# Sliding-window attention with a GELU feed-forward on one core: all output stores issued from ScalarE's queue

## The chip, the core and the metric

The kernel runs on one core of a Trainium2 chip. The metric is the device time of one execution in microseconds (us), the median of the runs. The profile is one execution on the same core, read by engine: TensorE (PE, with its weight loads PEld), VectorE (DVE), ScalarE (ACT), GpSimd (POOL) and the sync engine (SP), which computes nothing and only issues transfers. A `q` after an engine's name (SPq, ACTq) marks its instruction queue: issuing a transfer or waiting for one.

## What is computed

Attention over a causal window of 64 positions, for 8 batches of 8 heads, 576 positions and 64 elements per head; its output, taken as 4608 tokens of 512 elements, goes through a feed-forward layer with a quick GELU.

```python
scores = scale * np.matmul(q, k.transpose(0, 1, 3, 2))
mask = (rel >= 0) & (rel < window)                # rel = i - j, window = 64
attn = softmax(np.where(mask, scores, -1e9))
x = np.matmul(attn, v)  -> 4608 x 512
h = x @ w_in                                      # 512 x 2048
out = (h / (1.0 + np.exp(-1.702 * h))) @ w_out    # 2048 x 512, float32
```

## The kernel before, in words

The 4608 tokens are nine chunks of 512. A chunk's way is: q and k are loaded as bf16 (`load_bf16`, step `l`, on GpSimd's queue) and turned by a DMA transpose on the sync queue (`turn_dma`, step `y`, L240, two transfers `qt` and `kt` for each row block). TensorE makes scores (`c`, L319) into PSUM, ScalarE the exp (`x`, L333 or L335), VectorE the mask (`m`, L339), TensorE the product with v (`v`, L347), VectorE the normalised rows `xs` (`n`, L392). These are turned into `xT`, from chunk 4 on by a DMA transpose on the sync queue (`x_dma`, step `t`, L437).

The feed-forward layer then works in units `u` (L453): eight matmuls into one of two PSUM buffers `hps`, each emptied by ScalarE with a gelu (`.g`, L484) or, with a tanh first (`.t`, L464), by VectorE (`g`, L479). Since the same two buffers serve all units, TensorE is never more than two units ahead of ScalarE. The gelu and the exp need different tables on ScalarE; `soften` (L1089) and the first gelu after an exp bring a table load each.

The second matrix product is done for pairs of 128-token blocks with seven products instead of eight (`p`, L568): "chain" and "part" are its two PSUM banks, `k` copies a partial chain into SBUF (`keep_chain`, L113), `o` adds a half of an output row block into `o_sb` (`add_out`, L593, VectorE) and `z` copies the last half (`last_of_chain`, L113). `o_sb` has five buffers. When both halves are there, step `s` stores 128 rows of 512 float32 (256 KB, `store`, L584). In step names such as `s3.1` the first number is the pair (two to a chunk), the second the block in it; the last chunk has some stores in halves.

Chunks 0 and 1 are written out step by step; from chunk 2 on the order is the string `plan`, a list of such steps that the last lines of the kernel run one after the other. Each engine gets its own instructions in this order and works through them in order. Across engines only semaphores hold: one for each computing engine, and eight (DMAHW0 to DMAHW7) that the transfers of the sync queue and of ScalarE's queue use in turn. A transfer adds to its semaphore when it has landed. Before a transfer is issued, its queue waits for its data and for the landing of the transfer that had the same semaphore before, eight places earlier in the turn.

The plan around two of the stores, cut at the points:

```python
    u60.g p4.3 o4.3 a5.3 h4.1 a5.1 s3.1 l5.0 y4.2 h4.2 p4.4 z4.V x18 p5.1 ... k5.1.A u61.t ... p5.2 c19
    u93.g s6.0 p8.7 k8.7.V l6.4 p8.5 a8.4 c26 x26 c27.h x27 p8.4 ... y6.2 l7.1 z8.V p9.1 a9.1 s8.1 m26 y6.4 u94.t c28
```

The choice of queue is the first line of `store`: chunks below 6 and the second halves of the last chunk go to the sync queue, the others to ScalarE's. The stores of chunk 0 (`down_out`, L507) have a line of their own.

Of the kernel before, what the change touches and what calls it, by code (L numbers as in the profile page):

```python
# [29 lines left out]
def kernel(  # L30
# [9 lines left out]
    nc = tc.nc  # L40
# [538 lines left out]
        return o_of[c, pr, t][:, 256 * n : 256 * n + 256]  # L579

    def store(c, pr, t, half=None):
        eng = nc.sync if c < 6 or half == 1 else nc.scalar
        cols = slice(0, DM) if half is None else slice(256 * half, 256 * half + 256)
        eng.dma_start(  # L584
            out=out_tiled[:, 4 * c + 2 * pr + t, cols], in_=o_of[c, pr, t][:, cols]
        )
# [523 lines left out]
    def turn(m):  # L1110
# [15 lines left out]
        "o": lambda q, n: add_out(*pair(q), n),  # L1126
        "z": lambda q, e: last_of_chain(*pair(q), engines[e]),
        "s": lambda q, *t: store(*pair(q), *t),
        "a": lambda q, *n: add_g(*pair(q), *n),
        "w": add_w,  # L1130
# [48 lines left out]
```

The softmax here doesn't subtract the row's maximum and nothing guards it: scores larger than these inputs give would overflow.

## Time and profile before

| what | before |
|---|---|
| time, median of 3 runs (lowest, highest) | 295.31 us (294.74, 299.89) |
| span of the profiled execution | 293.0 us |
| ScalarE, gelu L484: 82 of them, mean | 597 ns |
| ScalarE, exp of 128x1024, L335: 28, mean | 1017 ns |
| ScalarE, table loads: 22, mean | 1283 ns |
| stores L584 on the sync queue: 22, median issue | 530 ns |
| stores L584 on ScalarE's queue: 12, median issue | 338 ns |
| DMA transposes on the sync queue: 80 | 60 at L240, 20 at L437 |

The page gives for each engine its busy time and share of the span. A list of waits says which instruction stood idle and what ended that, with total, times and longest in us. The timeline is a list of instructions with start and duration in us, and in brackets the idle time before one and what ended it. A line of the view by stages gives, after the length, the busy time of PE, PEld, DVE, ACT and POOL with the number of instructions, then the granted TensorE clock, the mean load of the 16 DMA engines (over 1 where packets of several queues are open on one engine at a time) and GB/s. Issuing a transfer is not counted as busy.

The 14 stores L584 issued before 205 us took 3.1 to 8.5 us from issue to landing; the 12 of ScalarE's queue, all after 246 us, 1.7 to 2.8 us.

### The profile page before, as it was taken

The page shows a single profiled execution, that of the slowest core. Times are in us where ns is not written, and L with a number is a line of the kernel's source. Part 1 is how long each engine was busy: PE and PEld are TensorE (multiplying, and loading weights), DVE is VectorE, ACT ScalarE, POOL GpSimd, SP SyncE. Part 2 cuts the span into 40 slices and gives each one's busy share as a digit, 9 for nine tenths or more (in the row PEclk, how much of TensorE's full clock was granted, in tenths as well). Part 3 has the DMA queues.
Part 4 walks back from the last instruction along what each step waited for, and adds up shares of the span by engine and source line. Part 5 has one row for each costly group of instructions (what it writes and reads, how often), then busy time and mean ns, then how long its engine had stood idle before and what let it go on. Part 6 is the DMA issues. An engine that isn't in the chain of part 4 may idle for free.

```text
span 293.0 us, 8976 instructions
## 1 busy us (share of the span) xinstructions
PE 283.5 (97%) x3783; PEld 249.6 (85%) x3783; DVE 195.5 (67%) x377; ACT 181.1 (62%) x289; POOL 141.3 (48%) x191
## 2 busy tenths in 40 slices
PE   7899999999999999999999999999999999999995
PEld 6578555999898898889898999998899899989984
DVE  5667715898898685375636573756787864768771
ACT  3676534877775389776758746776657653556411
POOL 1570446744999999709569985078510000000000
PEclk9999999999999999999999999999999999999999
DMA  7999999996999999999999999999955171001233
GB/s 237 236 206 219 240 243 225 239 159 128 84 142 119 166 130 134 185 164 146 140 186 154 139 151 198 183 160 143 142 70 117 36 182 39 0 2 72 74 125 126
DMA packets 149768, 42.79 MB, mean 146 GB/s; under 512 B 135136, under 2 KB 144864, under 8 KB 149728
## 3 DMA queue, kind: packets, MB, share of 16 engines
q0 software_dynamic: 77712, 13.64, 70.7%
q1 hardware_dynamic: 68208, 25.18, 49.4%
q10 hardware_dynamic: 3808, 3.41, 3.7%
q8 instruction: 29, 0.48, 0.7%
q14 instruction: 11, 0.09, 0.1%
HBM read 36.70 MB, written 9.44 MB: 157 GB/s over the span
## 4 chain that ended last, share of the span: by engine, by line
PE 78%; DMA 10%; DVE 4%; ACT 2%; SPq 2%; issue 2%; POOL 1%; ACTq 0%; DVEq 0%; POOLq 0%
PE hps L453 32%; PE chain L568 17%; PE part L568 13%; PE ops L491 5%; PE up L668 4%; DMA out_dram<-o_sb 3%; PE Tacc L347 3%; PE S L319 3%; DMA kt<-rows_k 3%; DMA stage_v<-in_v_dram 2%; DMA stage_qk<-in_k_dram 2%; SPq L240 1%; DVE stage_qk L528 1%; ACT PT L335 1%; PE turn L196 1%
## 5 line engine op out<-in xcount | busy, mean ns | idle before, releaser
L453 PEld LDWEIGHTS <-w_in_sb 128*128 128x128 bf16 x1312 | 109.6, 113 | 4.9 <-issue 0.7
L484 ACT ACTIVATE gT<-hps 128x512 bf16<-128x512 f32 x82 | 48.6, 597 | 34.5 <-PE hps L453 34.2
L453 PE MATMUL hps<-xT_pe,w_in_sb 128*128 128x128 bf16 (+2 forms) x800 | 61.0, 234 | 0.1
L453 PE MATMUL hps<-xT_dma,w_in_sb 128*128 128x256 bf16 x512 | 60.6, 273 | 0.3 <-ACT gT L694 0.3
L568 PEld LDWEIGHTS <-gT 128*128 128x128 bf16 x512 | 49.0, 98 | 5.9
L479 DVE SCALAR_TENSOR_TENSOR gT<-th,hps 128x512 bf16<-128x512 bf16 x46 | 30.8, 684 | 11.2 <-ACT th L464 11.0
L233 POOL COPY v_off<-v_nat 64x528 bf16<-64x528 bf16 x27 | 20.2, 752 | 33.9 <-DMA v_nat<-in_v_dram 33.1
L464 ACT ACTIVATE th<-hps 128x512 bf16<-128x512 f32 x46 | 27.0, 600 | 13.0 <-PE hps L453 12.6
L593 DVE TENSOR_TENSOR o_sb<-part,stage_v 128x256 f32<-128x256 f32 x48 | 20.2, 421 | 21.9 <-PE part L568 13.3
L335 ACT ACTIVATE PT<-S 128x1024 bf16<-128x1024 f32 x28 | 28.5, 1017 | 8.0 <-PE S L319 7.6
L339 DVE TENSOR_TENSOR PT<-PT,band_all 128x1024 bf16<-128x1024 bf16 x32 | 23.6, 748 | 5.6 <-ACT PT L335 5.4
L229 POOL DMA_DIRECT2D v_nat<-in_v_dram x27 | 23.5, 871 | 0.8 <-DMA rows_q<-in_q_dram 0.5
L228 POOL DMA_DIRECT2D rows_k<-in_k_dram x27 | 23.3, 865 | 0.3 <-DMA v_nat<-in_v_dram 0.3
L228 POOL DMA_DIRECT2D rows_q<-in_q_dram x27 | 23.1, 856 | 0.0
L568 PEld LDWEIGHTS <-sums 128*128 128x128 bf16 x192 | 18.6, 98 | 3.2 <-issue 1.1
L568 PEld LDWEIGHTS <-stage_v 128*128 128x128 bf16 x192 | 18.5, 98 | 2.2
L113 ACT COPY stage_v<-chain 128x256 f32<-128x256 f32 x22 | 8.2, 372 | 18.3 <-PE chain L568 18.3
L392 DVE TENSOR_TENSOR xs<-Tacc,rc 128x128 bf16<-128x128 f32 (+1 forms) x26 | 18.0, 692 | 0.9
L113 DVE COPY stage_v<-chain 128x256 f32<-128x256 f32 x26 | 10.9, 420 | 11.1 <-PE chain L568 10.9
L235 POOL COPY v_off<-v_nat 64x528 bf16<-64x528 bf16 x21 | 17.2, 820 | 1.2
L568 PE MATMUL chain<-stage_qk,sums 128*128 128x256 bf16 x128 | 16.6, 273 | 0.3 <-DVE stage_v L113 0.3
L568 PE MATMUL chain<-stage_qk,gT 128*128 128x256 bf16 x128 | 16.6, 273 | 0.0
(127 smaller groups left out, 450.6 us busy)
## 6 DMA issues: line engine op xcount, KB each, us to landing
out_dram<-o_sb SPq DMA_DIRECT2D x24, 256.0 KB, 4.7
rows_q<-in_q_dram POOLq DMA_DIRECT2D x21, 128.0 KB, 6.3
rows_k<-in_k_dram POOLq DMA_DIRECT2D x21, 128.0 KB, 6.7
v_nat<-in_v_dram POOLq DMA_DIRECT2D x21, 128.0 KB, 7.4
out_dram<-o_sb ACTq DMA_DIRECT2D x10, 256.0 KB, 2.1
stage_v<-in_v_dram SPq DMA_DIRECT2D x9, 256.0 KB, 6.7
stage_qk<-in_q_dram SPq DMA_DIRECT2D x4, 512.0 KB, 6.9
stage_qk<-in_k_dram SPq DMA_DIRECT2D x4, 512.0 KB, 8.0
```

The lines of the kernel that those rows point to most:

```text
L113: (nc.scalar.copy if engine is nc.scalar else engine.tensor_copy)(**kw)
L228: nc.gpsimd.dma_start(out=heads(row_block(b, i, w)), in_=rows_of(src, b, i))
L229: nc.gpsimd.dma_start(out=v_nat[b % 2][0 : size(i), i, :, 0:D], in_=rows_of(v, b, i))
L233: nc.gpsimd.tensor_copy(out=vo[64:128, i, :, :], in_=vn[0:64, i, :, :])
L335: nc.scalar.activation(out=e[:], in_=st[:], func=AF.Exp, scale=scale)
L339: nc.vector.tensor_tensor(out=pt, in0=pt, in1=band_all[:], op=ALU.mult)
L453: nc.tensor.matmul(ps[:, g, :], lhsT=w_in[:, c, (f + g) % 4 : 512 : 4], rhs=xT[ch][:, m0 : m0 + nt // P, c, :], start=(c == 0), stop=(c == 3),
L464: nc.scalar.activation(out=th[:], in_=ps[:], func=AF.Tanh, scale=1.702)
L479: nc.vector.scalar_tensor_tensor(out=g_of(*unit), in0=th[:], scalar=1.0, in1=ps[:], op0=ALU.add, op1=ALU.mult,)
L484: nc.scalar.activation(out=g_of(*unit), in_=ps[:], func=AF.Gelu_apprx_sigmoid, scale=2.0)
L568: nc.tensor.matmul(out[:, :], lhsT=left[:, j], rhs=right[:, j], start=new and j == 0, stop=j == 7, skip_group_check=True,)
L593: nc.vector.tensor_tensor(out=out_half(c, pr, t, half), in0=C_of[c, pr][:], in1=kept(c, pr, at), op=ALU.add)
```

## The change

All stores of step `s` are issued from ScalarE's queue. The place of each store in the plan is as it was, and the stores of chunk 0 (L507) stay on the sync queue. The sync queue is then left with loads and transposes, so that no transpose stands behind a store that waits for its data, and the stores have a queue of their own on the DMA engines.

```diff
     def store(c, pr, t, half=None):
-        eng = nc.sync if c < 6 or half == 1 else nc.scalar
+        eng = nc.scalar
         cols = slice(0, DM) if half is None else slice(256 * half, 256 * half + 256)
         eng.dma_start(
             out=out_tiled[:, 4 * c + 2 * pr + t, cols], in_=o_of[c, pr, t][:, cols]
```

In the built kernels the instructions of TensorE, VectorE and GpSimd are the same and in the same order. ScalarE has 22 transfers more among its instructions, the sync engine 22 fewer. The turn of the eight semaphores changes with it; the listing of ScalarE's instructions in the changed build has, for instance, for the stores of s3.1, s6.0, s8.1 and s8.0:

```
L584 DMACopy out_dram<-o_sb 128x512 [waits DMAHW7_49,Activation_49]
L584 DMACopy out_dram<-o_sb 128x512 [waits DMAHW4_49]
L584 DMACopy out_dram<-o_sb 128x512 [waits DMAHW5_49,DVE_49]
L584 DMACopy out_dram<-o_sb 128x512 [waits DMAHW6_49,DVE_49]
```

By the values waited for, the transfers eight places before them are the first transposes of y4.2 and y6.4 for s3.1 and s6.0, the second of y6.4 for s8.1, and the first of y7.1 for s8.0.

## The prediction

> **What bounds the kernel now.** I read the page's first part for the busy shares, then busy time by stage, then the waits of TensorE, and only then the sync queue and ScalarE in time.
>
> ```profile
> PE 283.5 (97%) x3783; PEld 249.6 (85%) x3783; DVE 195.5 (67%) x377; ACT 181.1 (62%) x289; POOL 141.3 (48%) x191
> ```
>
> TensorE is busy 97% of the span, ScalarE 62%. By stage (core line: length, then busy us of each engine):
>
> ```profile
> 100.00:140.00 40.00, 39.44 (x568) 35.84 (x569) 25.16 (x49) 30.25 (x46) 29.99 (x38) 1.00 2.10 155
> 140.00:180.00 40.00, 39.88 (x493) 36.80 (x491) 23.06 (x45) 26.86 (x41) 32.72 (x41) 1.00 2.03 161
> 180.00:220.00 40.00, 39.51 (x529) 36.01 (x527) 27.57 (x55) 27.20 (x40) 17.24 (x22) 1.00 1.42 142
> ```
>
> In these 120 us, where 14 of the moved stores lie, TensorE is idle for 0.56 + 0.12 + 0.49 = 1.2 us. So nothing there can be won by more than that, and any time TensorE is made to wait is added to the end. Its waits, all of them:
>
> ```profile
> PE S L319 <- DMA kt<-rows_k: 0.5, 1, 0.5
> PE part L568 <- DVE o_sb L593: 0.5, 1, 0.5
> ...
> PE hps L453 <- ACT gT L694: 0.3, 1, 0.3
> ```
>
> So today ScalarE holds TensorE up almost never; it is ScalarE that waits (34.2 us at L484 and 12.6 us at L464 for `hps`). The question is how late ScalarE may become before that turns round.
>
> **What the skill says.** "DMA: Bandwidth & Descriptors", section "Issuing engines are not separate DMA queues": transfers from any engine run on the same 16 DMA engines, so another queue saves only the issuing time. The trace agrees as far as it goes: a store's issue took 530 ns on the sync queue and 338 ns on ScalarE's (medians of L584), the bytes are the same. "Perfetto Trace Analysis", section on the HWDGE DMA instruction: the wait for semaphores is the sequencer's, and lies before the reported start. That matters most here: a store that waits holds the whole instruction stream of its engine. The sync queue's waits show it (one L584 store sat 28.7 us behind a transfer, harmlessly).
>
> **The change, part by part.** Twenty-two stores leave the sync queue for ScalarE's; twelve were there. No work is added or removed on TensorE, VectorE, GpSimd.
>
> *Issuing.* 22 x 338 ns = 7.4 us on ScalarE. Its 181.1 us become 188.5 of some 293, and it has gaps of 0.28 us before most gelu steps. Bounds: 0 (all in gaps) to 7.4 us (all exposed). Most stores stand where ScalarE waits for TensorE afterwards anyway, so I take 1.0 us.
>
> *New waits.* In the built program each transfer of sync and ScalarE counts on one of eight landing semaphores in turn and waits for the transfer that used it before. The listing of the changed build puts the moved stores later in this turn than in step order: step s3.1 waits for the first transpose of y4.2, step s6.0 for the first of y6.4, though both follow them in the plan. Before, the store was issued first. I set each store's place on ScalarE (end of the instruction before it) against the time its data and its semaphore were ready in the trace of before. For 20 of 22 both were ready, or are ready after a wait already counted (s8.1 and s8.0 wait for the transposes just behind y6.4's first), or late by little at the tail. Two are not:
>
> ```profile
> 118.67 3.59 SPq L437 DMA_TRANSPOSE xT_dma<-xs  x2
> 122.35 0.53 SPq L584 DMA_DIRECT2D out_dram<-o_sb  x1
> 122.98 1.38 SPq L240 DMA_TRANSPOSE qt<-rows_q  x1
> ```
>
> First, s3.1 (the middle line; start, then duration). ScalarE reaches it when the gelu before ends, at 123.5:
>
> ```profile
> 122.91 0.60 ACT L484 ACTIVATE gT<-hps 128x512 bf16<-128x512 f32 x1 [0.28 <-PE hps L453]
> 123.52 1.28 ACT L1089 ACT_TABLE_LOAD   x1
> 124.81 0.20 ACT L1089 ACTIVATE gate<-gate 1x1 f32<-1x1 f32 x1
> 124.92 1.00 ACT L335 ACTIVATE PT<-S 128x1024 bf16<-128x1024 f32 x1
> ```
>
> Without the store ahead of it the y4.2 transpose starts at 122.3. The 30 qt transposes landed 2.3/5.7/8.6 us after issue (least, median, most), this one after 7.9. With 5.7 it lands at 128.0 and ScalarE stands still for 128.0 - 123.5 = 4.5 us (bounds: 1.1 with 2.3; 6.7 with 7.9). Behind it stand the table load, the exp of pair 18, the copy of chain 5.1, the tanh of unit 61. TensorE needs the exp first: scores 19 write the bank that it reads, and began at 127.81, while the exp ended at 125.92, a slack of 1.9. So TensorE loses 4.5 + 0.34 - 1.9 = 2.9 us (0 to 5.1).
>
> ```profile
> 181.27 1.29 SPq L240 DMA_TRANSPOSE kt<-rows_k  x1
> 184.71 0.33 SPq L584 DMA_DIRECT2D out_dram<-o_sb  x1
> 185.14 1.28 SPq L240 DMA_TRANSPOSE qt<-rows_q  x1
> ```
>
> Second, s6.0. It was issued at 173.7 on the sync queue; ScalarE comes to it at 181.6, after unit 93. The y6.4 transpose is the last line above. It stood behind the store of s8.1, which waited for VectorE until 184.7; now it can go at 182.6. With 5.7 us it lands at 188.3: ScalarE waits 6.7 us (2.3: 3.3; its own 7.5: 8.5). TensorE works on through the products of pairs 8 and 9 and scores 26 and 27 until unit 94, begun at 185.80, which needs the bank that the exp of pair 27 frees (first half done at 184.5): slack 1.3. Loss 6.7 + 0.34 - 1.3 = 5.7 us (2.3 to 7.5). The shift of the first loss moves ScalarE and the sync queue alike here, since that stretch of transposes starts from `xs` (L437, 176.2), which VectorE writes.
>
> *Buffers of o_sb.* s9.0 goes out at 222.7 instead of 220.7; z11 and o11.5 want its buffer at 223.8, and a store on ScalarE lands after 2.1 us (median; 1.7 to 2.8). So VectorE is late by about a microsecond and TensorE's product 11.3 (225.15) by some 0.5 us (0 to 1).
>
> *What is saved.* VectorE waited 3.9 us for s2.0's landing (issued 114.31, landed 8.4 us later behind transposes), which cost TensorE its 0.5; on ScalarE it goes at 111.5. And the kt wait of 0.5 at 204.3 falls away, as the sync queue runs ahead. Together -1.0 us (0 to -1.2, the idle time above).
>
> *Tail.* The last half stores wait in ScalarE's stream for VectorE (288.38), so the copy of z16 slips from 287.1 to 288.7 and the last copy, z17, from 289.7 to 289.8: +0.1.
>
> **Sum:** 2.9 + 5.7 + 1.0 + 0.5 - 1.0 + 0.1 = 9.2 us on 295.3: **304.5 us**, slower by 3.1%.
>
> **Rivals.**
> 1. *The transposes land in time.* Without 22 stores in the sync ring, transposes land nearer 2.3 us than 5.7. For it: the qt and kt transposes after 208.9 landed within 2.4 to 4.5 us of their issue, when GpSimd's loads were nearly done. Against: in the stages of the two waits these loads overfill the 16 DMA engines (the next to last figures above, 2.10, 2.03 and 1.42), and they stay. Losses 0 + 2.3, less 1.0: 296.6 us, no change.
> 2. *Faster.* The sync queue no longer stops behind stores that wait for VectorE, transposes come earlier, q, k and xT are never late. For it: 20.3 us of waits of L584 on VectorE. Against: TensorE waits 0.5 us for transposes in all. 295.3 - 1.0 = 294.3 us, not slower.
> 3. *ScalarE becomes the bound.* The blocks take their longest (5.1 + 7.5) and issuing half shows (3.7): 295.3 + 16.3 + 0.5 + 0.1 = 312 us. For it: 21 table loads of 1283 ns crowd just where stores stand. Against: 46.8 us of ScalarE's waiting for `hps` can take them up.
>
> **How the numbers follow.** Forecast (two blocks, each costing TensorE some us): 0.60. Rival 1: 0.25. Rival 2: 0.05. Rival 3: 0.10. Most of the forecast's own spread lies over 301.2 us (2%): 0.56; with rival 3, slower 0.66. Within 2%: rival 1, most of rival 2, the low end of the forecast, 0.32. Over 2% faster would need 5.9 us, of which TensorE has 1.2 idle in the middle: 0.02. The range, 296.5 to 311, takes in rival 1 and the forecast with its bounds, and leaves out rival 2 and the upper half of rival 3.
>
> **What would show it.** In the changed profile: a gap of ScalarE of about 4.5 us before the table load after unit 60 and of about 6.7 us after unit 93, ended by a qt transpose's landing; TensorE idle near 3 us at scores 19 and near 6 us at unit 94, and with these two its waits on ScalarE up from 0.3 to some 9 us. VectorE's 3.9 us wait on `out_dram` gone. Wrong, if ScalarE's gaps there stay under 2 us, or if they come and TensorE does not stop; if more than a third of the loss lies outside the two places, issuing or buffers were sized wrongly.

## The result, and the profile after

| | before | after |
|---|---|---|
| time, median (lowest, highest) | 295.31 us (294.74, 299.89) | 306.53 us (305.50, 307.39) |
| span of the profiled execution | 293.0 us | 303.8 us |

The ratio is 1.0371, with a 95% interval from 1.0298 to 1.0443: slower by 11.2 us. Here and below, medians and ranges are of all runs, ratios of fast runs alone, since some runs of a kernel take over 1.5% longer than its fastest. The forecast was 304.5 us. The busy shares of the page of the kernel after say where to look:

```profile
PE 284.4 (94%) x3778; PEld 250.2 (82%) x3783; DVE 196.3 (65%) x377; ACT 180.8 (60%) x289; POOL 138.4 (46%) x191
...
PEclk9999999999999999969999999999999999999999
```

TensorE's busy time is up by only 0.9 us, in a span that is 10.8 us longer: it stands idle. The second line is its granted clock in slices of 7.6 us; the lone 6 lies between 129 and 137 us. The same three stages as before (length, busy us of PE, PEld, DVE, ACT and POOL, then clock, DMA load and GB/s):

```profile
100.00:140.00 40.00, 33.48 (x457) 29.32 (x457) 20.54 (x40) 24.70 (x37) 30.25 (x40) 0.91 2.02 149
140.00:180.00 40.00, 40.00 (x519) 36.89 (x514) 23.60 (x45) 29.24 (x45) 27.80 (x37) 1.00 2.01 154
180.00:220.00 40.00, 37.72 (x511) 34.19 (x509) 23.77 (x48) 24.51 (x37) 19.88 (x25) 1.00 1.32 141
```

TensorE's idle time there is 6.5, 0.0 and 2.3 us instead of 0.6, 0.1 and 0.5, and the clock of the first stage is 0.91 instead of 1.00. The list of TensorE's waits names the cause (total, times, longest):

```profile
PE S L319 <- ACT PT L335: 5.7, 1, 5.7
PE hps L453 <- ACT PT L333: 2.5, 2, 2.3
...
PE S L319 <- DMA kt<-rows_k: 0.6, 1, 0.6
```

The first two are waits for ScalarE, at scores 19 and at unit 94. Next, ScalarE in time around the two stores (start, duration, and in brackets the idle time before):

```profile
124.37 0.60 ACT L484 ACTIVATE gT<-hps 128x512 bf16<-128x512 f32 x1 [0.28 <-PE hps L453]
131.54 0.34 ACTq L584 DMA_DIRECT2D out_dram<-o_sb  x1
131.91 1.28 ACT L1089 ACT_TABLE_LOAD   x1 [6.94 <-DMA qt<-rows_q]
...
133.31 1.00 ACT L335 ACTIVATE PT<-S 128x1024 bf16<-128x1024 f32 x1
...
188.78 0.60 ACT L484 ACTIVATE gT<-hps 128x512 bf16<-128x512 f32 x1 [0.28 <-PE hps L453]
192.77 0.34 ACTq L584 DMA_DIRECT2D out_dram<-o_sb  x1
193.14 1.28 ACT L1089 ACT_TABLE_LOAD   x1 [3.76 <-DMA qt<-rows_q]
```

The gelu of unit 60 ends at 124.97, and nothing runs on ScalarE until the store of s3.1 goes out at 131.54: 6.9 us between the gelu and the table load (the store's own issue of 0.34 included), ended by a qt transpose. The transposes behind which the two stores wait were issued here (sync queue; start, then duration of the issue), the first right behind the `xT_dma` pair:

```profile
120.14 3.59 SPq L437 DMA_TRANSPOSE xT_dma<-xs  x2
123.83 1.26 SPq L240 DMA_TRANSPOSE qt<-rows_q  x1
...
189.24 1.19 SPq L240 DMA_TRANSPOSE qt<-rows_q  x1
```

(The line of 123.83 is the first transpose of y4.2, that of 189.24 the first of y6.4.) They landed at 131.5 and 192.75 us, 7.6 and 3.5 us after their issue. And what it does to TensorE:

```profile
127.67 1.04 PE L568 MATMUL part<-w_out_sb,gT 128*128 128x256 bf16 x8
134.36 0.61 PE L319 MATMUL S<-qt,kt 64*128 64x64 bf16 x16 [5.66 <-ACT PT L335]
134.90 1.89 PE L568 MATMUL chain<-stage_qk,stage_v 128*128 128x256 bf16 x8
```

Eight matmuls of 128x256 take 1.04 us ahead of the stop of 5.66 us and 1.89 us behind it: half rate.

To see where the 10.8 us arise I subtract the start of each matmul in the trace of before from that of the same matmul in the trace of after. This lag is 0.8 us at 123 us. It becomes 7.8 over scores 19 (127.81 before, 134.36 after, and 1.3 us more at half rate) and 10.3 over unit 94 (185.80 and 196.07). It falls to 9.7 at 204 us of before, where only the kernel before waits for kt, and stays there until the last products. The tail adds 1.1. So 7.0 + 2.4 of the 10.8 us arise at the two places that the prediction named.

A lag of 1.1 us is there before the first moved store goes out, at 112.1 us: TensorE waits 0.8 us for `v_off` at 77.9 us and 0.6 us for kt at 105.4 us (the last line of the list). In a second trace of the kernel after the lag at that point is 0.0, so these waits are not the work of the change.

### The profile page after: what moved, and what is told of

The parts are those of the page before. It is cut to its first block, busy times and chain, and to the rows that moved or that the text cites. A ratio compares the mean times of both kernels' runs of the same rounds, so it can differ in the third digit from the quotient of the medians.

```text
span 303.8 us, 8955 instructions
## 1 busy us (share of the span) xinstructions
PE 284.4 (94%) x3778; PEld 250.2 (82%) x3783; DVE 196.3 (65%) x377; ACT 180.8 (60%) x289; POOL 138.4 (46%) x191
## 4 chain that ended last, share of the span: by engine, by line
PE 76%; DMA 11%; ACT 3%; DVE 3%; POOL 2%; issue 2%; ACTq 1%; SPq 0%; DVEq 0%; POOLq 0%
PE hps L453 34%; PE chain L568 15%; PE part L568 11%; PE ops L491 5%; PE up L668 4%; DMA qt<-rows_q 4%; PE Tacc L347 3%; PE S L319 3%; DMA kt<-rows_k 3%; DMA stage_v<-in_v_dram 2%; DMA stage_qk<-in_k_dram 2%; DVE stage_qk L528 1%; ACT PT L335 1%; POOL v_off L101 1%; PE turn L196 1%
## 5 line engine op out<-in xcount | busy, mean ns | idle before, releaser
L464 ACT ACTIVATE th<-hps 128x512 bf16<-128x512 f32 x46 | 27.0, 599 | 11.2 <-PE hps L453 10.8
L233 POOL COPY v_off<-v_nat 64x528 bf16<-64x528 bf16 x27 | 19.8, 737 | 21.9 <-DMA v_nat<-in_v_dram 20.9
L319 PEld LDWEIGHTS <-kt 64*128 64x128 bf16 x576 | 10.6, 96 | 12.5 <-issue 10.7
L319 PE MATMUL S<-qt,kt 64*128 64x64 bf16 x576 | 14.4, 192 | 6.5 <-ACT PT L335 5.7
```

What stands on the lines that cost most here:

```text
L233: nc.gpsimd.tensor_copy(out=vo[64:128, i, :, :], in_=vn[0:64, i, :, :])
L319: nc.tensor.matmul(st[h % 2][:, t * 256 + hp * 64 : t * 256 + hp * 64 + 64], lhsT=src[1][part, hp, 64 * j : 64 * j + 128], rhs=src[0][part ...
L464: nc.scalar.activation(out=th[:], in_=ps[:], func=AF.Tanh, scale=1.702)
```

## The experiments

Theory A is that of the prediction: two stores on ScalarE's queue stand behind transposes that haven't landed, and all behind them on ScalarE stands too. The rivals: the issuing and the other twenty stores cost the time; or the stop matters less than the half clock that follows; or, later, the two blocks aren't two separate costs.

### One store alone, each way

```diff
-        eng = nc.sync if c < 6 or half == 1 else nc.scalar
+        eng = nc.sync if (c < 6 or half == 1) and (c, pr, t) != (1, 1, 1) else nc.scalar
```

> The kernel before with one store alone moved, s3.1, to ScalarE's queue. In its build that store waits for the first transpose of y4.2, as in the changed kernel. Theory A (two stores wait on ScalarE for transposes that share their landing semaphore): nearly the whole first loss, about 7 us, of which 5.7 is TensorE standing idle and 1.3 running at half clock after it: 301.5 to 303.5 us. Theory B (each store costs ScalarE its issuing time, 11.2 us over 22 stores, 0.5 each): 295.8 us. Theory C (stores in a queue of their own slow the loads and transposes beside them): one store of 256 KB, under 1 us: 295 to 296.

302.95 us (301.82 to 305.18) against 296.13 us of before: ratio 1.0219 (1.0150 to 1.0288). One store in another queue costs 6.8 us. Its waits, of TensorE and of ScalarE:

```profile
PE S L319 <- ACT PT L335: 5.5, 1, 5.5
```

```profile
ACT L1089 <- DMA qt<-rows_q: 6.7, 1, 6.7
```

The wait is the one of the kernel after; so it needs none of the other 21 moved stores.

The same for s6.0 (`(3, 0, 0)` in place of `(1, 1, 1)`):

> The kernel before with one store alone moved, s6.0, to ScalarE's queue. Here the turn of the eight semaphores comes out differently: the transfer eight places before it is an older store, which in the trace of before had landed at 176.6, 5 us before ScalarE gets there (181.6). Theory A: no wait, no loss, 294.5 to 296. If the place on ScalarE alone mattered and not the semaphore: 2 to 3 us slower, 297.5 to 298.5. Theory B: 295.8. Theory C: 295 to 296.

296.05 us (293.76 to 300.84) against 296.13: ratio 0.9991 (0.9963 to 1.0018). Alone on ScalarE's queue this store gets another place in the turn of semaphores; by the listing of the build the transfer eight places before it is an old store. ScalarE goes straight on:

```profile
181.36 0.60 ACT L484 ACTIVATE gT<-hps 128x512 bf16<-128x512 f32 x1 [0.28 <-PE hps L453]
182.23 0.60 ACT L484 ACTIVATE gT<-hps 128x512 bf16<-128x512 f32 x1 [0.28 <-PE hps L453]
182.24 0.36 ACTq L584 DMA_DIRECT2D out_dram<-o_sb  x1
182.85 1.28 ACT L1089 ACT_TABLE_LOAD   x1
```

Same engine, same place in the plan, same data: without the transpose ahead of it in the turn the store is free. So it is not the issuing, and not the store as such.

### All stores but the four that wait

The stores of s8.1 and s8.0 stand behind transposes issued just after that of s6.0; left on ScalarE they would take over its wait, so they go back as well.

```diff
-        eng = nc.scalar
+        eng = nc.sync if (c, pr, t) in ((1, 1, 1), (3, 0, 0), (4, 0, 1), (4, 0, 0)) else nc.scalar
```

> The changed kernel with four stores, s3.1, s6.0, s8.1 and s8.0, on the sync queue again; 18 of the 22 moved stores stay on ScalarE's. By the trace of before, no store on ScalarE then waits long for its semaphore. Theory A: the two gaps of ScalarE and both stops of TensorE are gone; what is left is the tail (1 us) and under 1 us of issuing: 295.5 to 298. Theory B: 18/22 of 11.2 us stay: 304.5. Theory C: the same 304 to 305.

297.43 us (294.01 to 301.97) against 296.13: ratio 1.0018 (0.9987 to 1.0049). Eighteen moved stores, with all their issuing, buffers and tail, cost 0.5 us by the ratio (-0.4 to 1.5) and 1.3 us by the medians, which can't be told from nothing. The rest of the loss is in four stores.

### All stores on ScalarE, four of them elsewhere in the plan

s3.1 goes behind s3.0 (some 10 us earlier), s6.0 behind s4.1, s8.1 and s8.0 behind unit 98:

```diff
-        m15 s2.0 s3.0 m14 ...   a5.3 h4.1 a5.1 s3.1 l5.0 ...
+        m15 s2.0 s3.0 s3.1 m14 ...   a5.3 h4.1 a5.1 l5.0 ...
-        ... u87.g v24 s4.1 a8.2 ... u93.g s6.0 p8.7 ... a9.1 s8.1 m26 ... x28 s8.0 m27 ... u97.g u98.g m28
+        ... u87.g v24 s4.1 s6.0 a8.2 ... u93.g p8.7 ... a9.1 m26 ... x28 m27 ... u97.g u98.g s8.1 s8.0 m28
```

> All stores on ScalarE's queue as in the changed kernel, but four steps stand elsewhere in the plan: s3.1 right after s3.0, s6.0 right after s4.1, s8.1 and s8.0 after unit 98. In the build the transfers eight places before them have landed when ScalarE gets there, by the trace of before. Theory A: 295 to 297.5, the queue itself costs next to nothing. Theory B and theory C: nothing changes, 305 to 308.

297.08 us (295.92 to 301.33) against 296.13: ratio 1.0041 (1.0012 to 1.0070). The queue itself is cheap once no store meets an open transfer; but the change as it was meant brings nothing either. In this trace three stores in a row were slow to issue on ScalarE:

```profile
113.75 2.88 ACTq L584 DMA_DIRECT2D out_dram<-o_sb  x3
```

They took 0.37, 0.69 and 1.63 us of issue, against the 0.34 of one that stands alone; behind them TensorE stopped for 2.0 us and then ran at half rate for 3.4. I tried s3.1 between units 55 and 56 instead, the rest as above:

> As the kernel in which four steps stand elsewhere in the plan (all stores on ScalarE's queue, none waiting long), but s3.1 stands after unit 55, not right behind s2.0 and s3.0. There three issues in a row (0.37, 0.69 and 1.63 us) held up the exp and TensorE's unit 54 by 2 us. If issuing in a row was what cost: no such wait of TensorE, 0.5 to 2 us less, 295 to 296.5, like the kernel before. If issuing costs the same anywhere: 297.

297.35 us (295.17 to 303.06) against 296.29: ratio 1.0049 (1.0017 to 1.0081). No better. But the wait was not gone: the two stores still in a row took 0.36 and 1.35 us of issue, and TensorE stopped for 1.0 us instead of 2.0. So the third issue in a row is not what kept the reordered kernel slower than before; whether the other two are, and what else is, stays open.

### The change once more, and without its first block

> The changed kernel itself once more, so that the next three stand beside it on one chip. 305 to 308 us, about 10.5 us over the kernel before.

307.95 us (303.69 to 310.16) against 296.29: ratio 1.0409 (1.0322 to 1.0496). In another set of runs the change costs about the same; the four runs lie so far apart that the 11.7 us of the medians is rough.

```diff
-        eng = nc.scalar
+        eng = nc.sync if (c, pr, t) == (1, 1, 1) else nc.scalar
```

> The changed kernel with s3.1 alone on the sync queue again. In its build s6.0 still waits for the first transpose of y6.4. Theory A (the first stop of TensorE and the half clock after it gone, the second stop of 2.4 us and the tail of 1 us left): 298.5 to 300. If the second stop is made up for later: 296 to 297.5. If each store costs its share: 21/22 of the loss left, 306.

307.53 us (306.39 to 309.50): ratio 1.0377 (1.0299 to 1.0455). A clear miss: theory A had the first block gone and with it most of the loss, 298.5 to 300 us. The first block was gone, and the second had grown. ScalarE and TensorE:

```profile
193.35 0.34 ACTq L584 DMA_DIRECT2D out_dram<-o_sb  x1
193.72 1.28 ACT L1089 ACT_TABLE_LOAD   x1 [7.56 <-DMA qt<-rows_q]
```

```profile
189.54 1.04 PE L568 MATMUL chain<-w_out_sb,gT 128*128 128x256 bf16 x8
196.65 1.87 PE L453 MATMUL hps<-xT_dma,w_in_sb 128*128 128x256 bf16 x8 [6.07 <-ACT PT L333]
```

ScalarE waits 7.6 us at s6.0, not 3.8; TensorE stands 6.1 us, not 2.3, and runs at half rate afterwards (1.87 us for eight matmuls). So each block's cost depends on the other. The opposite kernel, the first block alone among the moved stores (s6.0, s8.1 and s8.0 on the sync queue):

> The kernel after with s6.0, s8.1 and s8.0 back on the sync queue; s3.1 stays on ScalarE, so only the first long wait is left in the plan. Theory A, each long wait costs by itself what TensorE loses behind it: the first block costs what it did alone (302.95 against 296.13, 6.8), and the rest of the moved stores about 1: 303 to 304.5, TensorE stopped 5 to 6 us near 128 and no stop of over 1 us near 186 to 196. Theory B, the two blocks share one sum (a later first block only takes away what the second would cost), so that one alone costs as much as both: 306 to 308 here as well, with some other stop in the place of the second. Theory C, the second block is the dear one and the first is nearly free: 297 to 300.

301.84 us (299.85 to 304.08) against 296.57: ratio 1.0201 (1.0099 to 1.0302). The median is a little under theory A's figures, and outside those of B and C, though one of the four runs (299.85) is in C's. Nothing stops TensorE near 190 us; only the first block is left:

```profile
PE S L319 <- ACT PT L335: 4.2, 1, 4.2
```

So: first block alone 5.3 us (6.8 with s3.1 as the only moved store), second without the first 11.2, both 11.2 and 11.7. They don't add up. The first is rough: in the five traces with the same instructions ahead of it, ScalarE's wait at s3.1 was 5.4 to 6.9 us.

### What the half clock costs

In these kernels matmuls that are not part of the computation fill TensorE's gaps; ScalarE still waits. First the gap before scores 19 only:

```diff
-        h4.4 y4.3 p5.2 c19 g61 ...
+        h4.4 y4.3 p5.2 B100 c19 g61 ...
+        "B": lambda n: warm(n, psT, "T"),
```

> The changed kernel with 100 extra matmuls of 128x128 by 128 (work that nobody reads, into a free bank) on TensorE between product 5.2 and scores 19, where it stood idle for 5.7 us. ScalarE's wait stays as it was. If idling is what halves TensorE's granted clock there: no half-clock stretch, some 1.3 us less than the changed kernel, about 305. If the half clock has another cause, or if it costs nothing: the same as the changed kernel, or up to 1 us more where the extra matmuls outlast the wait. If ScalarE's wait were not what holds TensorE up, the extra 5.5 us would come on top: 311 to 312.

306.92 us (306.14 to 310.55): ratio 1.0374 (1.0281 to 1.0467). No gain. The trace shows that the filling kept the clock up where it stood:

```profile
127.67 5.75 PE L702 MATMUL idle<-ident 128*128 128x128 bf16 x100
133.35 0.41 PE L319 MATMUL S<-qt,kt 64*128 64x64 bf16 x16
133.69 1.05 PE L568 MATMUL chain<-stage_qk,stage_v 128*128 128x256 bf16 x8
```

Full rate after the gap (0.41 and 1.05 us, not 0.61 and 1.89). But ScalarE's wait in this execution was 5.4 us and not 6.9, so the exp of pair 18 ended at 131.9 us, and the filler held scores 19 up for 1.4 us more: about what the full rate saved. Then ScalarE waits 4.5 us at s6.0 instead of 3.8, TensorE stops for 3.0 us, and the half rate comes there: the lag grows by 5.9 us at the second place instead of 2.4. With both gaps filled (`B60` before unit 94):

> The kernel after with matmuls on TensorE that are not part of the computation put into both of its gaps (100 of 128x128 before scores 19, some 5.7 us; 60 before unit 94, some 3.4 us), so that it isn't idle in either for 3 us or more. If half-rate stretches after the stops are part of the cost (2.3 us behind the first block in the trace after, 2.5 behind the second when only the first gap was filled): none near 130 to 140 nor near 193 to 203, and 303.5 to 305. If what is saved in one place comes back as a longer wait in the next: 306 to 308, the saving given back at the kt wait or later.

305.39 us (305.15 to 306.26): ratio 1.0316 (1.0254 to 1.0378). Stages behind the two places, of this kernel:

```profile
134.00:142.00 8.00, 8.00 (x126) 7.43 (x124) 4.83 (x10) 5.63 (x10) 7.86 (x11) 1.00 2.53 150
197.00:205.00 8.00, 8.00 (x88) 7.44 (x85) 5.74 (x11) 5.59 (x9) 0.12 (x1) 1.00 1.79 179
```

Compare with the kernel after, behind the first place:

```profile
134.00:142.00 8.00, 7.64 (x95) 6.41 (x95) 4.45 (x10) 5.38 (x9) 7.86 (x11) 0.78 1.77 117
```

The clock stays at 1.00, against 0.78. (Behind unit 94 the kernel after ran at full rate too.) The kernel is 8.8 us slower than before, where the change was 11.2 and 11.7. From these medians the half clock would be 2 to 3 us of the loss; but the intervals overlap, 305.39 is just above the range expected, and the first filler again outlasts the exp, by 0.9 us. The traces give it directly, as what the lag grows by beyond the stop itself: 1.3 us at scores 19 in the kernel after (1.2 to 2.0 in the four traces with half rate there), and at unit 94 0.2 us in the kernel after, without half rate, and 2.8 to 2.9 us in three others with it. So by its trace the half clock is 1.3 us of what the change costs, and the standing still is the greater part.

The same filler in the second gap alone, with s3.1 on the sync queue:

> The kernel after with s3.1 back on the sync queue (first long wait gone) and 60 matmuls that are not part of the computation before unit 94 (some 3.4 us of the second gap). Against the run with s3.1 back alone (307.53): if the second stop there cost 6.1 us of waiting and 2.6 us of half rate, the filling takes the 2.6 away: 304.5 to 305.5. If the half rate does not come from the idle time (but, for instance, from what is moved at that time), no change: 307 to 308 with the half-rate stretch still there.

Undecided: 300.12 to 309.40 us in four runs, median 306.60. In its trace ScalarE waited 8.6 us at s6.0, and a wait of 3.8 us of TensorE and half rate for 3.4 us were left behind the filler, so it was too short for its purpose.

### Why the second block shrinks behind a first

Two explanations are left: a loss of time near 128 us lets the DMA queues get ahead, whatever causes it; or it has to do with where s3.1 is issued. This kernel has s3.1 on the sync queue, so no first block, and 100 matmuls that are not part of the computation in its place (the edits of the two diffs above together).

> The kernel after with s3.1 back on the sync queue, as in the run with s3.1 back alone (307.53), and in place of the first block 100 matmuls of 128x128 on TensorE that are not part of the computation, before scores 19: TensorE loses 5.7 us there without any store waiting on ScalarE. Theory A, a loss of time near 128 us, whatever its cause, lets the loads and transposes of the queues run ahead, and so shortens the second wait: ScalarE's wait at s6.0 is 3 to 5.5 us instead of 7.6 and 8.6, the DMA load from 180 to 190 about 1.4 to 1.7 instead of 1.9 to 2.1, and the time is 305 to 308.5, no more than without the 100 matmuls. Theory B, the second wait is set by something else than the time lost before it (s3.1 on the sync queue itself, for instance): the wait stays 7 to 9 us and the time is 307.5 + 5.7 = 312 to 314.

308.16 us (306.46 to 309.91) against 294.54: ratio 1.0426 (1.0352 to 1.0500). It spends 5.7 us on the filler that the kernel with s3.1 back does not, and ends 0.6 us later, where theory B wanted 312 to 314. Against the runs of before beside each it loses 13.6 us instead of 11.2 (theory B: 16.9): by the medians over half of the 5.7 us is made up. ScalarE:

```profile
195.04 0.34 ACTq L584 DMA_DIRECT2D out_dram<-o_sb  x1
195.41 1.28 ACT L1089 ACT_TABLE_LOAD   x1 [5.33 <-DMA qt<-rows_q]
```

5.3 us instead of 7.6, within theory A's 3 to 5.5. One part of its expectation failed: the DMA load from 180 to 190 us is 2.33, not lower. The load in a fixed stretch of 10 us may be the wrong measure, since everything lies later. I looked afterwards at the order of GpSimd's loads and the awaited transpose. Loads of the kernel after, and of the one with s3.1 back (start, duration):

```profile
181.96 0.88 POOL L229 DMA_DIRECT2D v_nat<-in_v_dram  x1 [5.46 <-issue]
182.82 0.89 POOL L228 DMA_DIRECT2D rows_q<-in_q_dram  x1
183.69 0.90 POOL L228 DMA_DIRECT2D rows_k<-in_k_dram  x1
184.55 0.91 POOL L229 DMA_DIRECT2D v_nat<-in_v_dram  x1
```

```profile
183.56 0.88 POOL L229 DMA_DIRECT2D v_nat<-in_v_dram  x1 [0.28 <-issue]
184.67 0.88 POOL L228 DMA_DIRECT2D rows_q<-in_q_dram  x1 [0.24 <-DMA rows_k<-in_k_dram]
186.60 0.88 POOL L228 DMA_DIRECT2D rows_k<-in_k_dram  x1 [1.05 <-DMA v_nat<-in_v_dram]
187.47 0.88 POOL L229 DMA_DIRECT2D v_nat<-in_v_dram  x1
```

In the kernel after, the last load of this group goes out 4.7 us before the transpose of y6.4 (189.24) and lands at 191.4; the transpose takes 3.5 us. With s3.1 back it goes out 0.9 us after the transpose (186.59) and lands at 197.3; the transpose, among these loads, takes 6.7. With the 100 matmuls the last load is 4.3 us ahead again (185.25 against 189.58), and the transpose takes 5.4. The other four traces with this wait agree: the transpose takes 2.8 to 4.6 us where the last load is 4.4 to 4.9 us ahead (the kernel after once more, first gap filled, both gaps filled), and 7.0 where it is 0.5 us ahead (s3.1 back, second gap filled). That time lost earlier shortens the second wait is shown by the last kernel, in its time and in one trace; that the loads standing ahead of the transpose are how, is read from seven traces and wasn't tried by itself.

How far TensorE's lag against the trace of before grows over each place, in us (from 127 to 160 us of before, and from there to 200; the filler's own 5.7 and 3.5 us, and half rate, included):

| kernel | over scores 19 | over unit 94 | ScalarE's wait at s6.0 |
|---|---|---|---|
| after | 7.0 | 2.4 | 3.8 |
| after, once more | 6.8 | 1.9 | 3.2 |
| s3.1 alone on ScalarE | 7.4 | 0.0 | none |
| s6.0, s8.1, s8.0 back | 5.4 | 0.0 | none |
| s3.1 back | 0.1 | 8.9 | 7.6 |
| s3.1 back, second gap filled | 0.4 | 8.9 | 8.6 |
| first gap filled | 5.4 | 5.9 | 4.5 |
| both gaps filled | 5.5 | 3.3 | 4.6 |
| s3.1 back, 100 matmuls instead | 5.4 | 6.7 | 5.3 |

The traces of three of them (s3.1 alone; s3.1 back; the last) carry 3.1 to 4.5 us of lag into the first place. In the first and the last most of it arises at about 80 us, where TensorE waited 2.1 to 2.2 us for `v_off` and ran at half rate behind it; with s3.1 back 1.7 us come from the first 20 us, 1.9 from this wait and 1.0 from near 105 us. No edit touches that, and the wait is there in some executions only, so the table counts growth over the places. It may be what spreads the runs of before from 293 to 302 us; that isn't shown.

## Why the prediction was right, step by step

The time and its direction were right, and the mechanism was the one predicted, at the places predicted. The sum came closer than its terms, and that is luck: the first block was priced 4.1 us too low, the second 3.3 us too high and the tail 1.0 us too low.

*The mechanism.* "s3.1 waits for the first transpose of y4.2, step s6.0 for the first of y6.4": so it was, with the releaser the prediction named on both table loads, and TensorE stopped at scores 19 and unit 94. The Trainium skill's "Perfetto Trace Analysis", in the section on the HWDGE DMA instruction, has the wait of an issued transfer in the sequencer ahead of its reported start; the trace agrees: the store of s3.1 is reported as 0.34 us at 131.54, and the 6.9 us appear as idle time of the table load behind it. Whoever looks for long stores sees nothing.

*First block, 2.9 us: too small.* The step that failed is the landing time, 5.7 us, the median of all qt transposes; here it was 7.6, as it had been in the trace of before (7.9). "Without the store ahead of it the y4.2 transpose starts at 122.3": it started at 123.8, the `xT_dma` pair still before it, but ScalarE too came 1.5 us later than assumed (124.97 for 123.5), so this changed nothing. ScalarE waited 6.9 us, the store's issue included, and TensorE stopped for 5.7, the slack being 6.94 - 5.66 = 1.3 us for 1.9. So 1.9 us of the error are the landing, 0.6 the slack, and most of the rest is the half rate of the next paragraph. The transfer's own time in that stage was the figure to take, and the median over all stages was not.

*The term that was missing.* The Trainium skill's "TensorE: Matmul & The Clock Gate", Part 1: The HAM clock gate, says that after an idle window of about 3.4 us TensorE runs at half rate until it has been busy for some time. I priced the stop at its own length. The kernel after, from the start of the stop on:

```profile
128.70:130.70 2.00, 0.00 (x1) 0.02 (x1) 0.00 (x0) 0.00 (x0) 0.00 (x0) 1.00 1.90 170
130.70:134.36 3.66, 0.00 (x0) 0.00 (x0) 0.00 (x0) 2.44 (x4) 2.65 (x4) 0.50 1.04 204
134.36:137.50 3.14, 3.14 (x29) 2.26 (x29) 1.96 (x4) 2.96 (x4) 3.14 (x5) 0.50 1.43 122
```

The trace agrees with the page in that half rate came with a stop of 5.7 us. But it began 2.0 us into the stop, sooner than a whole idle window of 3.4 us would allow. It lasted 6.8 us, of which TensorE worked 3.1, and 1.3 us of its lag came with it.

*Second block, 5.7 us: too large, and for the reason that mattered most.* It was 2.4 us. "The shift of the first loss moves ScalarE and the sync queue alike here" failed: the time lost near 128 us moved ScalarE and TensorE, but, as far as the order of the loads shows, let the loads get ahead of the transposes; this one landed in 3.5 us and not 5.7. It was also issued 0.1 us before ScalarE came to the store, not 1.0 us after. The two, 2.2 and 1.1 us, make up the error. Without the first loss the same store cost 8.9 us in the trace, more than I gave it. I added two costs that take from each other; the alternative, worked out from each block alone, is 5.3 + 11.2 = 16.5 us, and the kernel lost 11.2.

*Issuing 1.0, o_sb buffers 0.5, saved -1.0: 0.5 in all.* 0.5 us measured with the four waiting stores back (0.9987 to 1.0049), the tail included. In the trace of after TensorE's lag grows by 0.3 us at 115 us, behind the issues of s2.0 and s3.0. VectorE's wait of 3.9 us on `out_dram` is gone and TensorE got 0.65 back at 123 us; the kt wait at 204 us is gone too, another 0.5. So the saving came, 1.2 us. VectorE has a new wait on `out_dram`, 0.9 us at 250.5 us; but between 214 us and the last products the lag is constant, so s9.0's buffer cost TensorE nothing.

*Tail, 0.1: it was 1.1 us.* The copy of z16 stood behind stores in ScalarE's stream, and then a last copy and a last store had to follow. Of the 1.1 us, 0.45 are the later issue of that store and 0.63 its landing, which took 2.4 us and not 1.7:

```profile
296.47 2.03 ACTq L584 DMA_DIRECT2D out_dram<-o_sb  x3
298.60 0.37 ACT L113 COPY o_sb<-chain 128x256 f32<-128x256 f32 x1 [4.89 <-DMA out_dram<-o_sb]
299.00 0.82 ACTq L584 DMA_DIRECT2D out_dram<-o_sb  x2
299.92 0.37 ACT L113 COPY o_sb<-chain 128x256 f32<-128x256 f32 x1 [0.95 <-PE chain L568]
300.32 0.34 ACTq L584 DMA_DIRECT2D out_dram<-o_sb  x1
```

In other kernels with these stores on ScalarE the tail was 0.5 to 1.4 us.

*The rivals.* Transposes that land in time, and a gain, are refuted: ScalarE's gaps are 6.9 and 3.8 us and TensorE stopped. ScalarE as the bound is refuted by the eighteen stores that cost 0.5 us.

## What to carry to other kernels

Before a transfer is moved to the queue of a computing engine, list everything that its issue waits for in the built program, the semaphore that it shares with an unrelated transfer included; on a queue that only moves data such a wait may be free (28.7 us in one case here, with nothing behind it but two stores whose data came 18 us later still), in a computing engine's stream all work behind it stands. Price the wait by the landing time of that very transfer in that stage (7.9 and 7.5 us in the trace of before; 7.6 at the first place, 6.7 and 7.0 at the second where no first stop came ahead of it), and add the half clock behind a long stop of TensorE. Two stalls in one stream are not to be added: time lost at the first changes what is in flight at the second, so remove each alone and both together before saying which is the cause.

## What the runs showed of the hardware

- Half rate comes behind some stops of TensorE that are shorter than the window of 3.4 us in the Trainium skill's "TensorE: Matmul & The Clock Gate", Part 1: 3.0 us in the kernel with the first gap filled, and 2.0 to 2.2 us in four other traces (three stores in a row, and `v_off`). Length alone doesn't decide: stops of 2.2 us (s3.1 back), 2.3 us (the kernel after) and 3.1 us (s3.1 behind unit 55, at 211.6 us) brought none. Where it came, it lasted 3.4 or 6.8 us.
- Whether a queue of their own makes the stores land sooner is not settled. s2.0 and s3.0 took 8.0 and 9.0 us from issue to landing on ScalarE's queue, 8.5 and 8.4 on the sync queue. The 13 stores before 208 us took 4.1 us in the median in the kernel after, and 14 took 7.2 before, but they were issued at other moments; with the four waiting stores back, the nine left on ScalarE's queue took 8.3. The Trainium skill's "DMA: Bandwidth & Descriptors", section "Issuing engines are not separate DMA queues", says that all queues share the DMA engines; the times with the four stores back agree.
- A store issued close behind another on ScalarE's queue took longer to issue than the 0.34 us of one alone: 0.39 to 0.74 us in most cases, and 1.15 to 1.78 at times (0.37, 0.69 and 1.63 us for three in a row; 0.34, 1.64 and 0.44 at 256 us in the kernel after). Why some take so long wasn't tried.
